# Weight gradients of the MLP run between the matmuls of the backward convolution, with the transposed tables and k^T kept in DRAM

## The chip, the cores and the metric

The kernel runs on one core of a Trainium2 chip. The time is the device time of one execution in microseconds (us), and runs are compared by their median.

## What is computed

Two layers are applied twice with the same weights: A, a gated long convolution, and B, an MLP. The kernel returns the output and the gradients for q, k, v, the short filter `shift_k`, the long filter `ssm_k`, `ssm_D`, and both weights and biases of the MLP.

```python
def _A_ref(q, k, v, shift_k, ssm_k, ssm_D):          # S = 2048, D = 512
    for t in range(4):
        k_shift = k_shift + k_pad[:, t:t + S, :] * shift_k[:, 3 - t][None, None, :]
    kv = k_shift * v
    y = irfft(rfft(pad(kv)) * rfft(pad(ssm_k)))[:S]   # length 2S, along the sequence
    return q * (y + kv * ssm_D)
def _B_ref(x, w1, b1, w2, b2):                        # F = 1376
    return gelu(x @ w1 + b1) @ w2 + b2
x = A_q
x = x + _A_ref(layernorm(x), A_k, A_v, A_shift_k, A_ssm_k, A_ssm_D)
x = x + _B_ref(layernorm(x), B_w1, B_b1, B_w2, B_b2)  # both lines a second time
_out, _vjp = jax.vjp(_f, A_q, A_k, ..., B_b2);  _grads = _vjp(grad_out)
```

Both uses of A share k, v and the filters, so the convolved y is computed once, and its gradient (`gy`) is the sum over both layers. The weight gradients of the MLP are sums over both layers as well: dW2 = h^T G and dW1 = (gz^T n)^T, where h, gz, G and n are kept per layer.

## The kernel before

**Stages in order.** `phase_conv_forward` makes the cosine and sine tables (`tabN`, `tabF`), transforms the filter and kv in five groups of frequencies, multiplies the spectra and transforms back to `res.y`; it keeps the spectra in DRAM (`Hspec`, `KVspec`). `phase_mlp` runs the two layers forward and then backward in four slices of 512 rows, and leaves in DRAM the tiles h and gz of both layers (11 chunks of 128 by 2048) and the normed inputs n. It then calls `weight_grads`. Last comes `phase_conv_backward`.

**Weight gradients, L897 to L934.** Both n are loaded whole (`dw_n`, 2 MB each, L906). For each of 22 chunks the tile `dw_tm` of each layer is transposed by a DMA (L920) and 32 matmuls of 128x512 run into one accumulator (L925). ScalarE evicts it (L928). For dW1 the result is turned by a DMA transpose (L933) and stored. There are 704 matmuls in all, and nothing else runs on TensorE meanwhile.

**Backward convolution.** The gradient `gy` is folded on VectorE (L174 to L205) and transformed with 112 matmuls (L230, table `tabFb`). For each group the spectrum `Hb` is loaded, multiplied on VectorE (L242 to L251) and transformed back with the table `tabIb` (L278 and L281, 112 matmuls). The table is made by four DMA transposes (L481). `inv_blocks` (L295 to L309) combines the blocks on VectorE into `gkv`. A loop over four blocks of 512 rows multiplies by v and by the shifted k, stores the gradient of v, loads 64 shifted tiles `kj` of k (L549 to L554, 128 KB each), runs 64 matmuls `gw` for the gradient of the short filter (L557) and transposes gks on TensorE (L562, evicted at L565). 256 small matmuls `gk` (L581) give the gradient of k, stored tile by tile (L585). Then `tabG` comes by four DMA transposes (L594), GY is multiplied by `KVb`, 228 matmuls `gh` (L627 and L629) transform back, and `inv_blocks` and two more operations for each of four column chunks give the gradient of the long filter, stored at L649. The last store is the small `gdo` (L651).

**What sets the order.** Tiles come from pools; a scheduler places the instructions on each engine, and an engine takes its own in that order. All DMAs of these stages are issued from one queue, SyncE's (SP), in order: a DMA that waits for its data or its buffer holds back all that stand behind it. A pool that opens where another was closed waits for the last use of that memory.

## Time and profile before

| what | before |
|---|---|
| median of 3 runs | 1245.59 us (1244.38 to 1254.66) |
| profiled execution: time | 1254.15 us |
| profiled execution: span | 1252.4 us |
| mean granted clock of TensorE | 0.829 |
| PE busy in the span | 789.9 us (63%) |
| VectorE (DVE) busy | 672.1 us (54%) |
| ScalarE (ACT) busy | 433.3 us (35%) |
| DMA traffic | 191.07 MB, mean 153 GB/s |

Each execution is profiled with times of every instruction from the span's start. Of the profiled execution 1.75 us lie outside the span. The granted clock is a share of full speed: 0.50 and 1.00 stand for TensorE's two levels, 1.2 and 2.4 GHz. The DMA share of a stretch is the mean busy share of the core's 16 DMA engines; it can exceed 1 a little at the edges of a short stretch.

### The profile page before, as it was taken

The numbers are of one execution on the slowest core, as the hardware profiler recorded it, in microseconds if no ns is written. First come the engines' busy times: TensorE is split into PE (matmuls) and PEld (weight loads), VectorE is DVE, ScalarE is ACT, GpSimd is POOL, SyncE is SP. The second block draws the span as 40 slices with busy tenths as digits, with TensorE's granted clock in tenths as the row PEclk, the third lists the DMA queues.
The fourth block names the chain that finished last, engine by engine and source line by source line (L and its number), as shares of the span: only waits on it lengthen the run. The fifth ranks groups of instructions, "written<-read, shape, count | busy, mean of one in ns | idle before, by whom it ended". The sixth has DMA issues, their size and how long they took to land. (4 is left out here: it accounts for less than half of the span.)

```text
span 1252.4 us, 10780 instructions
## 1 busy us (share of the span) xinstructions
PE 789.9 (63%) x3765; PEld 353.5 (28%) x3765; DVE 672.1 (54%) x1316; ACT 433.3 (35%) x538; POOL 97.5 (8%) x173
## 2 busy tenths in 40 slices
...
GB/s 193 138 227 165 172 163 69 79 146 113 135 143 147 155 143 193 185 202 207 206 233 169 168 131 44 220 173 171 172 189 133 159 118 34 135 244 219 140 18 50
DMA packets 308402, 191.07 MB, mean 153 GB/s; under 512 B 192814, under 2 KB 299260, under 8 KB 307964
## 3 DMA queue, kind: packets, MB, share of 16 engines
...
## 5 line engine op out<-in xcount | busy, mean ns | idle before, releaser
L816 PE MATMUL o_ps<-w_sb,h_sl 128*128 128x512 bf16 x352 | 96.0, 415 | 33.6 <-DVE h_sl L785 33.6
L925 PE MATMUL dw_ps<-G,dw_tm 128*128 128x512 bf16 x352 | 80.3, 393 | 42.2 <-issue 36.4
L257 DVE COPY spec_rb<-Hb 128x512 bf16<-128x512 bf16 x1 | 0.3, 294 | 197.6 <-DMA Hb<-Hspec_d 197.6
L925 PEld LDWEIGHTS <-dw_tm 128*128 128x128 bf16 x704 | 69.6, 99 | 128.8 <-issue 42.3
L835 PE MATMUL gh_ps<-gT_sl,w2T_sb 128*128 128x512 bf16 x352 | 85.0, 394 | 20.1 <-DMA gT_sl<-G 16.4
L803 PE MATMUL z_ps<-nT_sl,w_sb 128*128 128x512 bf16 x352 | 82.9, 390 | 19.5 <-DMA nT_sl<-n_sl 19.1
L846 PE MATMUL gn_ps<-w1T_sb,gz_sl 128*128 128x512 bf16 x352 | 83.5, 384 | 0.0
L891 ACT ACTIVATE nb_sl<-nb_sl,ab_ab 128x512 bf16<-128x512 bf16 x32 | 23.4, 802 | 152.5 <-DVE bb_junk L849 116.8
L925 PE MATMUL dw_ps<-dw_n,dw_tm 128*128 128x512 bf16 x352 | 76.1, 379 | 0.0
L928 ACT ACTIVATE dw_o<-dw_ps 128x512 bf16<-128x512 f32 x22 | 13.1, 597 | 181.9 <-PE dw_ps L925 181.9
L837 DVE SCALAR_TENSOR_TENSOR gz_sl<-gh_ps,gpb 128x512 bf16<-128x512 f32 x88 | 58.5, 689 | 25.9 <-DMA gpb<-gp_d 17.8
L805 ACT ACTIVATE g_z<-z_ps,b1col 128x512 bf16<-128x512 f32 x88 | 54.3, 691 | 19.8 <-PE z_ps L803 19.7
L816 PEld LDWEIGHTS <-h_sl 128*128 128x128 bf16 x352 | 33.8, 104 | 85.4 <-DVE h_sl L785 40.1
L813 PE MATMUL o_ps<-x_sl,ident 128*128 128x512 bf16 x32 | 13.3, 414 | 67.3 <-DVE x_sl L762 64.2
L835 PEld LDWEIGHTS <-w2T_sb 128*128 128x128 bf16 x352 | 35.4, 101 | 64.7 <-DMA gT_sl<-G 15.3
L803 PEld LDWEIGHTS <-w_sb 128*128 128x128 bf16 x352 | 34.8, 100 | 65.0 <-issue 16.7
L739 ACT ACTIVATE n_sl<-x_sl,ln_nmr,rstd 128x512 bf16<-128x512 bf16 x32 | 24.7, 820 | 70.0 <-POOL ln_nmr L732 70.0
L557 PE MATMUL gw<-kj,gks 128*128 128x512 bf16 x64 | 26.5, 561 | 32.9 <-DMA kj<-kB_d 20.6
L846 PEld LDWEIGHTS <-gz_sl 128*128 128x128 bf16 x352 | 34.7, 99 | 40.6 <-issue 2.0
L781 ACT ACTIVATE g_s<-g_t 128x2048 bf16<-128x2048 bf16 (+1 forms) x24 | 42.5, 1772 | 9.3 <-DVE g_t L780 9.3
L778 ACT ACTIVATE g_q<-g_z 128x2048 bf16<-128x2048 bf16 (+1 forms) x24 | 42.9, 1787 | 0.1
L278 PE MATMUL iv_ps<-Yg,tabI 128*128 128x512 bf16 x56 | 19.5, 453 | 36.7 <-DVE Yg L243 33.2
...
## 6 DMA issues: line engine op xcount, KB each, us to landing
...
```

What stands on the lines that cost most here:

```text
L557: nc.tensor.matmul(gw[cc], lhsT=gks[:, 4 * i + h, cs], rhs=kj[:, :, cs], start=(i == 0 and h == 0), stop=(i == 3 and h == 3))
L739: nc.scalar.activation(out=n[:, t, :], in_=x[:, t, :], func=ACT.Identity, bias=nmr[:, t:t + 1], scale=rstd[:, t:t + 1])
L778: nc.scalar.activation(out=q, in_=zb, func=ACT.Square)
L781: nc.scalar.activation(out=sg, in_=t, func=ACT.Sigmoid)
L803: nc.tensor.matmul(ps, lhsT=w.w1[:, dc, c * P:(c + 1) * P], rhs=nT[:, dc, :], start=(dc == 0), stop=(dc == ND - 1))
L805: nc.scalar.activation(out=zb[:, c - c0, :], in_=ps, func=ACT.Identity, bias=w.b1col[:, c:c + 1])
L816: nc.tensor.matmul(ps, lhsT=h[:, c, t * P:(t + 1) * P], rhs=w.w2[:, c, :], start=False, stop=(c == NFC - 1))
L835: nc.tensor.matmul(ps, lhsT=w.w2T[:, dc, c * P:(c + 1) * P], rhs=gT[:, dc, :], start=(dc == 0), stop=(dc == ND - 1))
L837: nc.vector.scalar_tensor_tensor(out=gz[:, c, :], in0=ps, scalar=1.0, in1=gp[:, c - c0, :], op0=ALU.mult, op1=ALU.mult, accum_out=m.b1part ...
L846: nc.tensor.matmul(ps, lhsT=gz[:, c, t * P:(t + 1) * P], rhs=w.w1T[:, c, :], start=(c == 0), stop=(c == NFC - 1))
L891: nc.scalar.activation(out=n[:, t, :], in_=n[:, t, :], func=ACT.Identity, scale=ab[:, 1, t:t + 1], bias=ab[:, 0, t:t + 1])
L925: nc.tensor.matmul(ps, lhsT=tm[:, i, t, :], rhs=rhs, start=(i == 0 and t == 0), stop=(i == 1 and t == NT - 1))
```

## The change

`weight_grads` becomes a generator, `fill`. It yields after each matmul with an estimate of that matmul's length. `conv_backward`, now a generator too, yields a number (`slack`) at places where TensorE would stand idle, and the driver then takes as many steps of `fill` as fit in it. What is left at the end runs after the convolution. TensorE's instructions of this part are wrapped so that the scheduler keeps them in the written order (`Ordered`).

The other parts of the change are these. The filler's tiles `dw_tm` are now one layer's each, with three buffers for each layer, and are fetched five ahead. n is loaded into G's memory once G has been used, so that the order of the work is all dW2 first. The transpose at the end of dW1 is four 128x128 matmuls and a second eviction. In the forward convolution the tables `tabI` and `tabG` and the transpose of k are written to DRAM, the last two by way of `res.y`'s memory. The backward part loads `tabIb`, `tabG` and `kTc` from there. The gradient of the short filter is 16 fused multiply-and-sum operations of 128x2048 on VectorE, and the 64 loads `kj`, the flipped copy `kB` and the 64 matmuls `gw` are gone. All DMAs of the backward convolution are issued from the GpSimd (Pool) queue, and SP keeps those of the weight gradients. `inv_blocks` works in place with two temporaries. The products by KV are made for all groups first, in place in GY, and `gh` runs column chunk by column chunk. Stores of gk are four tiles at a time.

```diff
...
-    flip_rows(nc, dram.kB, aps["A_k"].flatten_outer_dims(), 511, n=259)
     with ExitStack() as res.gystack:
-        phase_mlp(nc, tc, dims, consts, dram, res, aps)
+        m = phase_mlp(nc, tc, dims, consts, dram, res, aps)
         res.ystack.close()
         unflip_rows(nc, aps["out_0"].flatten_outer_dims(), dram.o0B)
         unflip_rows(nc, aps["out_1"].flatten_outer_dims(), dram.o1B)
-        phase_conv_backward(nc, tc, dims, consts, dram, res, aps)
+        dw = open_weight_grads(tc, res.gystack)
+        with ExitStack() as cst:
+            nc = Ordered(nc, tc, ("tensor",))
+            fill = weight_grads(nc, m, dims, aps, dw)
+            room = 0.0
+            for slack in conv_backward(cst, nc, tc, dims, consts, dram, res, aps):
+                room += slack
+                while room > 0.0:
+                    step = next(fill, None)
+                    room = room - step if step else 0.0
+            for _ in fill:
+                pass
...
+    nc.sync.dma_start(out=dram.tabI, in_=tabI)
+    tabG = res.y[:, :, :].rearrange("p (f k a) (b q) -> p f (k a b) q", f=2, a=1, q=256)
+    load_inverse_table(nc, tabG, dram.tabN)
+    nc.sync.dma_start(out=dram.tabG, in_=tabG)
+    kTn = res.y[:, :, :].rearrange("p (c t) d -> p c (t d)", c=ND)
+    for cc in range(ND):
+        nc.sync.dma_start_transpose(out=kTn[:, cc, :], in_=k_ap[:, cc * P:(cc + 1) * P])
+    nc.sync.dma_start(out=dram.kT, in_=kTn)
...
-def inv_blocks(nc, pool, W, N, last=False):
+def inv_blocks(nc, W, PN, MW, last=False):
 
     tt = nc.vector.tensor_tensor
-    G, B0, B1, PN, MW = [pool.tile([P, 2, 2, 512], BF16, name=f"ib{x}", tag=f"ib{x}", bufs=1)[:, :, :, 0:N]
-                         for x in range(5)]
     tt(out=PN, in0=W[:, :, 4:6], in1=W[:, :, 6:8], op=ALU.add)
     tt(out=MW, in0=W[:, :, 4:6], in1=W[:, :, 6:8], op=ALU.subtract)
+    G, B0, B1 = W[:, :, 4:6], W[:, :, 6:8], W[:, :, 2:4]
...
+    dma = nc.gpsimd.dma_start
...
-        nc.sync.dma_start(out=tabF, in_=dram.tabF)
+        dma(out=tabF, in_=dram.tabF)
         gyv = res.gy_bf[:, :, :].rearrange("p (i h) d -> p i (h d)", i=4)
         fg = Fold(nc, tp, gyv[:, :, 0:2 * D], gyv[:, :, 2 * D:4 * D], False)
+        yield 24.0
         for g, (k1, base, n) in enumerate(GROUPS):
             fwd_group(nc, psum, tabF, fg.streams(k1), g, GY[g])
...
+    tmp = res.gy_bf[:, :, :].rearrange("p (x a b) d -> p x a b d", x=4, a=2)
...
+        with tc.tile_pool(name="cb_rot", bufs=1, side="right") as rot:
+            tabI = rot.tile([P, 2, 16, 256], BF16, name="tabIb")
+            dma(out=tabI, in_=dram.tabI)
+            for g, (k1, base, n) in enumerate(GROUPS):
+                H = gyp.tile([P, 2, 4, 512], BF16, name="Hb", tag="Sg", bufs=2)
+                dma(out=H[:, :, 0:n, :], in_=dram.Hspec[:, :, base:base + n, :])
+                Rb = spec_second(nc, rot, H) if g == 0 else None
+                Y = rot.tile([P, 2, 4, 512], BF16, name="Yb", tag="Yg", bufs=1)
+                product(nc, rot, GY[g], H, Rb, g, Y, True)
+                yield 12.0 if g == 0 else 3.5
+                inv_group(nc, psum, tabI, Y, g, W)
         for m in range(2):
-            inv_blocks(nc, wp, W[m], 512)
-            tt(out=gkvv[:, :, m], in0=W[m][:, 0, 0:4], in1=W[m][:, 1, 0:4], op=ALU.add)
-            tt(out=gkvv[:, :, 2 + m], in0=W[m][:, 0, 0:4], in1=W[m][:, 1, 0:4], op=ALU.subtract)
-        wstack.close()
-        iostack = ExitStack()
-        io = iostack.enter_context(tc.tile_pool(name="cb_io", bufs=1))
-        gw = [psum.tile([P, 4, P], F32, name=f"gw{cc}", tag=f"gw{cc}", bufs=1) for cc in range(ND)]
-        gT = io.tile([P, ND, S + 16], BF16, name="gksT")
-        nc.vector.memset(gT[:, :, S:S + 16], 0.0)
-        for i in range(4):
-            sl = slice(4 * i, 4 * i + 4)
-            vb = io.tile([P, 4, D], BF16, name="vb", tag="vb", bufs=2)
-            tok_io(nc, vb, v_ap, dram.vB, i)
-            ksb = io.tile([P, 4, D], BF16, name="ksb_b", tag="ksb", bufs=2)
-            nc.sync.dma_start(out=ksb, in_=dram.ks[:, sl, :])
-            tt(out=gks[:, sl, :], in0=gkv[:, sl, :], in1=vb, op=ALU.mult)
-            tt(out=ksb, in0=gkv[:, sl, :], in1=ksb, op=ALU.mult)
-            tok_io(nc, ksb, out3, dram.o3B, i, store=True)
-            for h in range(4):
-                kj = io.tile([P, 4, D], BF16, name="kj", tag="kj", bufs=2)
+            inv_blocks(nc, W[m], tmp[:, 2 * m], tmp[:, 2 * m + 1])
+            tt(out=W[m][:, 0, 4:8], in0=W[m][:, 0, 0:4], in1=W[m][:, 1, 0:4], op=ALU.add)
+            tt(out=W[m][:, 1, 4:8], in0=W[m][:, 0, 0:4], in1=W[m][:, 1, 0:4], op=ALU.subtract)
+            yield 16.0
...
+                tok_io(nc, vb, v_ap, dram.vB, i, eng=nc.gpsimd)
+                ksb = io.tile([P, 4, D], BF16, name="ksb_b", tag="ksb", bufs=2)
+                dma(out=ksb, in_=dram.ks[:, 4 * i:4 * i + 4, :])
+                for h in range(4):
+                    gkv = W[h % 2][:, h // 2, 4 + i, :]
+                    tt(out=ksb[:, h, :], in0=gkv, in1=ksb[:, h, :], op=ALU.mult)
+                    tt(out=gkv, in0=gkv, in1=vb[:, h, :], op=ALU.mult)
...
+                yield 3.0
...
+                    dma(out=out2[(t - 3) * P:(t + 1) * P, :].rearrange("(t p) d -> p t d", p=P), in_=go)
+            gwo = io.tile([P, ND, 4], F32, name="gwo", tag="gwo", bufs=1)
+            junk = W[0][:, 0, 0:4, :].rearrange("p a d -> p (a d)")
+            for cc in range(ND):
...
+            for cc in range(ND):
+                kc = gyp.tile([P, 4096], BF16, name="kTc", tag="Sg", bufs=2)
+                nc.vector.memset(kc[:, 0:16], 0.0)
+                dma(out=kc[:, 16:16 + S], in_=dram.kT[:, cc, :])
...
-                for cc in range(ND):
-                    cs = slice(cc * P, (cc + 1) * P)
-                    nc.tensor.matmul(gw[cc], lhsT=gks[:, 4 * i + h, cs], rhs=kj[:, :, cs],
-                                     start=(i == 0 and h == 0), stop=(i == 3 and h == 3))
...
+                    nc.vector.scalar_tensor_tensor(out=junk, in0=gT[:, cc, 0:S], scalar=1.0,
+                                                   in1=kc[:, 16 - j:16 - j + S], op0=ALU.mult, op1=ALU.mult,
+                                                   accum_out=gwo[:, cc, j:j + 1])
+                    yield 1.6
+            gwb = wp.tile([P, ND, 4], BF16, name="gwb", tag="gwb", bufs=1)
+            nc.vector.tensor_copy(out=gwb, in_=gwo)
+            nc.scalar.dma_start(out=out4.rearrange("(c p) j -> p c j", p=P), in_=gwb)
...
-        for f in range(2):
-            for qt in range(2):
-                nc.sync.dma_start_transpose(out=tabG[:, f, :, qt * P:(qt + 1) * P], in_=dram.tabN[:, f, qt, :])
+        dma(out=tabG[:, :, :, 0:256], in_=dram.tabG)
...
+            KV = gyp.tile([P, 2, 4, 512], BF16, name="KVb", tag="Sg", bufs=2)
+            dma(out=KV[:, :, 0:n, :], in_=dram.KVspec[:, :, base:base + n, :])
+            Rb = spec_second(nc, hp, KV) if g == 0 else None
+            product(nc, hp, GY[g], KV, Rb, g, GY[g], True)
+            yield 1.3 * n
+        gdo = hp.tile([P, ND], BF16, name="gdo")
+        for cc in range(ND):
+            cs = slice(cc * P, (cc + 1) * P)
+            w = hp.tile([P, 2, 8, NQP], BF16, name="Wh", tag="Wh", bufs=2)
+            for g, (k1, base, n) in enumerate(GROUPS):
...
-            nc.sync.dma_start(out=out5[cc * P:(cc + 1) * P, :], in_=gh)
+            dma(out=out5[cc * P:(cc + 1) * P, :], in_=gh)
...
-        for i, l in ((0, 3), (1, 1)):
-            nc.sync.dma_start(out=nres[:, i, :, :], in_=m.n_d[l].rearrange("(t p) d -> p t d", p=P))
...
+    units = []
+    for which in range(2):
+        cs = list(range(NFC))
+        groups = [cs[:3]] + [[c] for c in cs[3:]] if which else [[c] for c in cs[:-3]] + [cs[-3:]]
+        for g in groups:
+            units += [(which, i, c) for i in range(2) for c in g]
+    tms, pss, late = {}, {}, []
+
+    def fetch(k):
+        which, i, c = units[k]
+        tms[k] = d.tp.tile([P, NT, P], BF16, name="dw_tm", tag=f"dw_tm{i}")
+        nc.sync.dma_start_transpose(out=tms[k], in_=(m.gz_d if which else m.h_d)[layers[i]][:, c, :])
+
+    def flush():
...
+    ahead = 5
+    for k in range(ahead):
+        fetch(k)
...
+    for k, (which, i, c) in enumerate(units):
+        if k + ahead < len(units):
+            fetch(k + ahead)
+        flush()
+        if which == 1 and (k == 0 or units[k - 1][0] == 0):
+            nc.sync.dma_start(out=m.G[1], in_=m.n_d[1].rearrange("(t p) d -> p t d", p=P))
+        f0, fcs = dims.FC[c]
+        if i == 0:
+            pss[c] = d.pp.tile([P, D], F32, name="dw_ps", tag="dw_ps")
+        ps, tm = pss[c], tms.pop(k)
+        for t in range(NT):
+            nc.tensor.matmul(ps, lhsT=tm[:, t, :], rhs=m.G[i][:, t, :], start=(i == 0 and t == 0),
+                             stop=(i == 1 and t == NT - 1))
+            yield 0.23
+        if which == 0 and i == 0 and c == NFC - 1:
+            nc.sync.dma_start(out=m.G[0], in_=m.n_d[3].rearrange("(t p) d -> p t d", p=P))
+        if i == 0:
+            continue
+        o = d.evp.tile([P, D], BF16, name="dw_o", tag="dw_o")
+        nc.scalar.activation(out=o, in_=ps, func=ACT.Identity)
+        if which == 0:
+            late.append((o[0:fcs, :], out9[f0:f0 + fcs, :]))
+        else:
+            pt = d.pp.tile([P, ND, P], F32, name="dw_pt", tag="dw_ps")
+            for dc in range(ND):
+                nc.tensor.matmul(pt[:, dc, :], lhsT=o[:, dc * P:(dc + 1) * P], rhs=m.ident, start=True, stop=True)
+            oT = d.evp.tile([P, ND, P], BF16, name="dw_oT", tag="dw_oT")
+            nc.scalar.activation(out=oT, in_=pt, func=ACT.Identity)
+            late.append((oT[:, :, 0:fcs], out7[:, f0:f0 + fcs].rearrange("(c p) f -> p c f", p=P)))
+            yield 0.3
...
```

Three places show how the order moves. The first is SP's queue in the forward convolution, where the inverse transform of kv needs `tabI` and, group by group, the filter's spectrum `Hg`; before:

```order
L481 DMA_TRANSPOSE tabI<-tabF_d 128x16x128 x4
L460 DMA Hg_997<-Hspec_d 128x2x1024
L463 DMA KVspec_d<-KVg 256x1x1024
L460 DMA Hg_1041<-Hspec_d 128x2x1024
L460 DMA Hg_1079<-Hspec_d 128x2x2048
L463 DMA KVspec_d<-KVg 256x1x1024
L460 DMA Hg_1182<-Hspec_d 128x2x2048
L463 DMA KVspec_d<-KVg 256x1x2048
L460 DMA Hg_1291<-Hspec_d 128x2x2048
L463 DMA KVspec_d<-KVg 256x1x2048 x2
L675 DMA w_sb<-in_B_w_dram 128x4x1376
```

And in the changed kernel (`y_res` is the memory of `res.y`, used as a buffer):

```order
L491 DMA tabI_d<-tabI 128x8192
L526 DMA_TRANSPOSE y_res<-tabN_d 128x16x128 x3
L507 DMA KVspec_d<-KVg 256x1x1024
L504 DMA Hg_1054<-Hspec_d 128x2x1024
L494 DMA tabG_d<-y_res 128x8192
L507 DMA KVspec_d<-KVg 256x1x1024
L504 DMA Hg_1092<-Hspec_d 128x2x2048
L497 DMA_TRANSPOSE y_res<-in_A_k_dram 128x2048 x4
L507 DMA KVspec_d<-KVg 256x1x2048
L498 DMA kT_d<-y_res 128x8192
L504 DMA Hg_1195<-Hspec_d 128x2x2048
L504 DMA Hg_1304<-Hspec_d 128x2x2048
```

Eleven transposes and stores that were not there stand on this queue; of the loads `Hg`, the first now goes ahead of the table (row 33 of the queue, not shown), and the later ones stand behind the transposes and stores of the two copies.

The second place is TensorE at the first inverse transform of the backward convolution (`iv_ps`). Before, it follows the forward transform (`sp_ps`) directly:

```order
L230 LDWEIGHTS tabFb
L230 MATMUL sp_ps<-fold_t,tabFb 128x512
L230 LDWEIGHTS tabFb
L230 MATMUL sp_ps<-fold_t,tabFb 128x512
L278 LDWEIGHTS tabIb
L278 MATMUL iv_ps<-Yb,tabIb 128x512
L278 LDWEIGHTS tabIb
L278 MATMUL iv_ps<-Yb,tabIb 128x512
```

In the changed kernel matmuls of the weight gradients (`dw_ps`, with G of one layer) stand before and after each group's inverse transform; here at its beginning:

```order
L55 LDWEIGHTS dw_tm
L55 MATMUL dw_ps<-G_3480,dw_tm 128x512
L55 LDWEIGHTS dw_tm
L55 MATMUL dw_ps<-G_3480,dw_tm 128x512
L55 LDWEIGHTS tabIb
L55 MATMUL iv_ps<-Yb,tabIb 128x512
L55 LDWEIGHTS tabIb
L55 MATMUL iv_ps<-Yb,tabIb 128x512
```

Every weight gradient matmul stood ahead of the backward convolution; now 73 of them stand ahead of its forward transform and 52 behind it, 61 between the five inverse groups, 139 behind the last of these, 52 between the transposes of gks, 194 between `gk` and `gh`, and 133 between and behind the four column chunks of `gh`.

The third place is where the gradient of k is stored and the last stage's loads are issued. Before, on SP's queue:

```order
L153 DMA out_dram<-o3B_d 4x256x512
L554 DMA kj<-kB_d 128x512 x4
L585 DMA out_dram<-gk_o 128x512 x3
L612 DMA KVb<-KVspec_d 128x2x2048
L585 DMA out_dram<-gk_o 128x512 x2
L612 DMA KVb<-KVspec_d 128x2x2048
L585 DMA out_dram<-gk_o 128x512 x3
L576 DMA out_dram<-gwb 128x4x4
L585 DMA out_dram<-gk_o 128x512 x3
L612 DMA KVb<-KVspec_d 128x2x2048
L585 DMA out_dram<-gk_o 128x512 x5
L594 DMA_TRANSPOSE tabG<-tabN_d 128x16x128 x4
```

In the changed kernel these stand on the Pool queue:

```order
L199 DMA out_dram<-ksb_b 128x2x512
L199 DMA o3B_d<-ksb_b 128x2x512
L199 DMA out_dram<-ksb_b 128x2x512
L199 DMA o3B_d<-ksb_b 128x2x512
L189 DMA out_dram<-o3B_d 4x256x512
L604 DMA out_dram<-gk_o 128x4x512 x2
L610 DMA kTc<-kT_d 128x2048 x2
L604 DMA out_dram<-gk_o 128x4x512 x2
L641 DMA KVb<-KVspec_d 128x2x1024 x2
L624 DMA tabG<-tabG_d 128x32x256
L634 IOTA nyq_i 1x272
L641 DMA KVb<-KVspec_d 128x2x2048 x3
```

The loads `kj` are gone, four loads `kTc` have come, each behind the VectorE work that frees its buffer, and the loads `KVb` and the plain load of `tabG` stand behind them.

## Rows read from the trace of the kernel before

**Rows 1.** Stretches: start:end, length, busy time of each engine, PE clock, DMA share, GB/s.

```profile
774.00:1236.00 462.00, 291.80 (x1540) 146.20 (x1540) 149.82 (x276) 83.76 (x136) 0.35 (x1) 0.80 0.62 147
790.00:805.00 15.00, 0.00 (x0) 0.00 (x0) 0.00 (x0) 0.00 (x0) 0.00 (x0) 0.50 1.06 307
850.00:900.00 50.00, 50.00 (x234) 22.64 (x232) 0.00 (x0) 4.68 (x8) 0.00 (x0) 1.00 0.81 170
900.00:950.00 50.00, 50.00 (x233) 22.64 (x232) 0.00 (x0) 4.18 (x7) 0.00 (x0) 1.00 0.99 190
972.00:1236.00 264.00, 135.52 (x836) 76.56 (x836) 149.41 (x275) 70.63 (x114) 0.35 (x1) 0.72 0.43 129
1050.00:1100.00 50.00, 12.22 (x55) 5.53 (x54) 33.08 (x44) 5.38 (x10) 0.00 (x0) 0.60 0.36 108
1100.00:1150.00 50.00, 27.83 (x160) 13.78 (x158) 5.34 (x5) 7.20 (x13) 0.00 (x0) 0.64 0.68 212
1236.00:1252.00 16.00, 0.00 (x0) 0.00 (x0) 0.00 (x0) 0.00 (x0) 0.00 (x0) 0.50 0.10 33
```

**Rows 2.** Groups of instructions from 740: line, form, count, busy, mean ns, idle before.

```profile
L925 PE MATMUL dw_ps<-G,dw_tm 128*128 128x512 bf16 x352 | 80.3, 393 | 42.2 <-issue 36.4 <-DMA dw_tm<-h_d 5.7
L925 PE MATMUL dw_ps<-dw_n,dw_tm 128*128 128x512 bf16 x352 | 76.1, 379 | 0.0
...
L557 PE MATMUL gw<-kj,gks 128*128 128x512 bf16 x64 | 26.5, 561 | 32.9 <-DMA kj<-kB_d 20.6 <-DMA kj<-in_A_k_dram 12.2
...
L627 PE MATMUL gh_ps<-tabG,Yh 128*128 128x257 bf16 x112 | 19.0, 288 | 12.9 <-DMA tabG<-tabN_d 12.4 <-ACT Wh L632 0.5
...
L581 PE MATMUL gk_ps<-wdiag_b,gksT 128*128 128x128 bf16 x256 | 18.5, 239 | 3.3 <-ACT gk_o L584 3.1 <-ACT gksT L565 0.2
...
L278 PE MATMUL iv_ps<-Yb,tabIb 128*128 128x512 bf16 x56 | 16.1, 404 | 8.9 <-DMA tabIb<-tabF_d 7.5 <-ACT Wb L284 1.4
...
L928 ACT ACTIVATE dw_o<-dw_ps 128x512 bf16<-128x512 f32 x22 | 13.1, 597 | 181.9 <-PE dw_ps L925 181.9
...
L250 DVE TENSOR_TENSOR pr_u<-GY,Hb 128x1024 bf16<-128x1024 bf16 x8 | 5.5, 690 | 0.0
...
L882 DVE SCALAR_TENSOR_TENSOR ab_u<-g_sl,ab_u 128x512 bf16<-128x512 bf16 x8 | 5.5, 688 | 0.0
...
L174 DVE TENSOR_TENSOR fold_x<-gy_bf 128x4096 bf16<-128x4096 bf16 x1 | 2.3, 2292 | 2.1 <-DMA out_dram<-dw_oT 2.1
```

**Rows 3.** SP's queue in order of time: start, length, issue, count.

```profile
775.10 15.59 SPq L906 DMA_DIRECT2D dw_n<-n_d  x2
790.73 24.34 SPq L920 DMA_TRANSPOSE dw_tm<-h_d  x6
...
1013.84 10.51 SPq L481 DMA_TRANSPOSE tabIb<-tabF_d  x4
...
1173.24 9.14 SPq L594 DMA_TRANSPOSE tabG<-tabN_d  x4
1214.30 21.45 SPq L649 DMA_DIRECT2D out_dram<-gh  x4
1235.86 0.38 SPq L651 DMA_DIRECT2D out_dram<-gdo  x1
```

**Rows 4.** The page, its groups: VectorE's longest idle time.

```profile
L257 DVE COPY spec_rb<-Hb 128x512 bf16<-128x512 bf16 x1 | 0.3, 294 | 197.6 <-DMA Hb<-Hspec_d 197.6
```

**Rows 5.** Stretches of the forward convolution, columns as in the first group.

```profile
139.00:156.00 17.00, 0.00 (x0) 0.00 (x0) 0.41 (x1) 1.00 (x1) 0.00 (x0) 0.60 1.08 212
...
170.00:190.00 20.00, 14.12 (x50) 5.22 (x51) 12.82 (x20) 6.14 (x6) 0.00 (x0) 0.83 0.38 136
190.00:210.00 20.00, 17.42 (x66) 6.85 (x65) 9.59 (x14) 8.31 (x10) 0.00 (x0) 0.84 0.25 101
210.00:224.00 14.00, 12.67 (x58) 5.32 (x57) 4.31 (x7) 8.31 (x10) 0.00 (x0) 0.98 0.00 1
```

**Rows 6.** Waits of SP's queue: for what, in total, times, longest.

```profile
SPq L1071 <- DMA out_dram<-gdo: 11.5, 1, 11.5
```

207 lines of the change are left out of this document (88 added, 119 removed).

## The prediction, made before the changed kernel ran

> **What bounds the kernel now.** I read the stretches first, from the point where the MLP's backward part ends (774) to the last store (1236). In these 462 us TensorE works 291.8 us and VectorE 149.8 us, and the DMA share is 0.62 [rows 1]. No unit is full over the whole; each is full in its own part. From 790 to 805 nothing computes and the DMAs run at 307 GB/s. From 850 to 950 TensorE is full at the high clock (1.00), DMA 0.81 to 0.99, VectorE 0. From 972 on it is the other way: in 264 us TensorE is busy 135.5 us at a mean clock of 0.72, and DMA is at 0.43. From 1050 to 1100 VectorE works 33 us and TensorE 12, from 1100 to 1150 TensorE 28 and VectorE 5, the DMAs at 212 GB/s [rows 1]. VectorE's longest idle time, 197.6 us, is the whole stage of the weight gradients [rows 4]: its next work needs memory and SP's queue, which that stage holds. The groups say what TensorE waits for there: 36.4 us at the start of the weight gradients ("issue"), 32.9 us for the loads `kj`, 12.4 us for `tabG`, 7.5 us for `tabIb` [rows 2]. SP's queue explains the first: two loads of 2 MB take 15.6 us before the first transpose is issued [rows 3]. So the tail is two stages in series, one full on TensorE and DMA, one a chain of waits with half of TensorE free.
>
> **What the change removes and adds, in work.** One weight gradient matmul costs 76.1/352 = 0.216 us at the high clock [rows 2]; 704 cost 152 us. The backward convolution's matmuls at that rate: 224 of 128x512 (forward and inverse) 48 us, `gk` 18.5 us at most [rows 2], `gt` 4 (64 with a quarter of the columns), `gh` some 25 (228 with half), the new turn of dW1 44 small ones, 3 us, and the sums for b2, 32 matmuls, 7: together 257 us, where 291.8 stand now. Gone are 64 `gw`, 26.5 us [rows 2]. TensorE waits 11 times for an eviction (0.60 us by L928 [rows 2]) before it turns dW1: 7 us. So TensorE alone would need about 265 us.
>
> VectorE gets 16 multiply-and-sums of 128x2048, for which no row stands. The nearest: the same operation on 128x512 takes 688 ns, a plain product of 128x1024 690 and of 128x4096 2292 [rows 2]. From the last two a plain product costs 0.155 us and 0.52 ns an element; the fused one then 1.04 ns an element, or 2.29 us for 2048. At the plain product's rate it would be 1.22 us, at four times the short one 2.75. I take 2.37 with the read of the sum: 38 us, between 20 and 44. VectorE has 149.8 + 38 = 188 us, still far below the tail.
>
> DMA: from 850 to 900, 234 matmuls use 14.6 transposed tiles, at a share of 0.81, so 2.8 us of all engines a tile, its stores with it; 44 tiles are 122 us. The loads of n cost 16 us (15 us at 1.06), the stores of the last MLP slices some 10. The convolution's own are 0.43 x 264 = 114 us [rows 1], less 64 `kj` (8 MB, about 26 us at 212 GB/s and share 0.68 [rows 1]), and with the table transposes (10.5 + 9.1 us [rows 3]) turned to plain loads of 2 MB, some 7 us each at 307 GB/s, plus 2 MB `kTc`: about 90. In sum some 240 us. This is close under the length that I get below; DMA isn't the bound, but every load will land late.
>
> **The chain of the changed tail, step by step from 774** (before's clock of the span). Fold and `tabFb`: five operations of 2.3 us [rows 2] make 12 us; the load of 2 MB shares the DMAs with five transposes and the last stores, and both are in after 23 us, at 797, with the sums for b2 and 73 weight gradient matmuls (23 us) as cover. Forward transform 112 x 0.216 = 24, to 821. `tabIb` can only be loaded when the forward transform leaves its memory: 7 us alone, double in company; 16, of which 52 matmuls (11 us) are cover: 837. The inverse transform and 61 matmuls, 37: 874. `inv_blocks`, two sets of six operations of 128x2048 and nine of 128x1024, about 27 us of VectorE, is covered by 139 matmuls, 30: 905. Four blocks of gks, each 16 small and 13 large matmuls (4 us) and a wait of some 7 us for the third and fourth block's loads, whose buffers come free late: 30, to 935. From here two routes run side by side: TensorE does `gk` (18.5 and some 5 waiting for stores), 194 matmuls, seven turns with their evictions, 48: 1006. VectorE does the multiply-and-sums, 38, and the products by KV, 31 (eight of 128x2048, some thirty of 128x1024), with some 10 us waiting because each `KVb` waits for a buffer that `kTc` or an earlier product holds, and `tabG` stands ahead of three of them on Pool's queue: 1014. The first column chunk ends just behind that, 1016. Three more, each 57 `gh` (6.3 us) and 29 matmuls (6.3): 38, to 1054. The last eviction, `inv_blocks` on the short rows (7 us: four stores stand 21.45/3 apart [rows 3]) and the store of `gh` (about 5): 14, to 1068. The remaining 46 matmuls and two turns take 12 and are done by then.
>
> Behind the last work 16.4 us stay: the store `gdo` goes at 1235.9 and its end is waited for 11.5 us [rows 3, 6]; the span ends at 1252.4. That gives 1084. For landings that come later than I have put them, with DMA at 80 per cent of the tail, I add 10.
>
> **The front pays.** Between 139 and 156 the DMAs are at 1.08 and TensorE idle, waiting for the first four transposes; after it their share falls to 0.38, 0.25 and 0.00, with TensorE at 14 of 20, 17 of 20 and 13 of 14 us [rows 5]. There is room for the work added: four transposes of a table like the first (15 us), four of k, three stores of 2 MB (7 us each at 307 GB/s, 10 at 212), about 50 us of DMA. But it stands on SP's queue ahead of loads `Hg` that the chain needs. The second `Hg` goes behind the four new transposes, some 15 us later, and the first now ahead of the table, some 3 earlier. Bounds: 0 (all in the gaps) and 50 (all in series). I take 10, because the gaps after 170 hold it and what TensorE does there has slack only in the first two groups. The copy of the flipped k (1 MB) is gone, which is in the 10.
>
> Sum: 1084 + 10 + 10 = 1104 of span, 1.75 us around it: 1106, against the profiled 1254.15, 12 per cent less. That execution lies above the median of the runs shown, 1245.59, so the changed median may lie a few us lower; I say 1105.
>
> **A rule weighed against it.** The rows show DMA at 0.81 to 0.99 while the weight gradients run and at 0.43 in the convolution [rows 1]; two queues can fill that valley, but not raise the peak. The Trainium skill, "DMA: Bandwidth & Descriptors", section on issuing engines, says as much: DMAs from any engine run on the same 16 engines, and a second issuer saves only issue time. By it, the Pool queue speeds no load up, and the overlap pays in late landings. What that comes to, priced from rows, is rival (a).
>
> **Rivals.** (a) DMA is the bound. Transposes that share the engines with 2 MB loads land at half rate; `tabFb`, `tabIb`, the block loads, the `KVb` and the last tiles `dw_tm` each come 10 to 12 us later than in my chain, and since TensorE's order is fixed, nothing passes them: five places, +50, 1155. For it: 0.99 from 900 to 950. Against: the same rows keep TensorE full with it [rows 1].
> (b) TensorE alone bounds the tail: 774 + 265 + 14 + 16 and a front of 5 give 1074. For it: the filler is cut to the gaps. Against: at 1014 VectorE's route is already the longer.
> (c) The front costs 40 rather than 10, all else equal: 1136.
> (d) Slower. Pool's DMAs, some 45 where SP had them, each need Pool to make them up; if one costs Pool 4 us and they go one after another on the chain, that is 180 us and undoes the 150 saved; it decides from about 3.4 us apiece. SP issues in 0.3 to 0.6 us, and for Pool there is no row. 1265. Against: about a dozen stand on the chain, 48 us by that price. The Trainium skill, "SBUF — State Buffer", section on who interferes with whom, speaks for (d): DMAs issued from GpSimd are held up while VectorE runs copies or tensor-scalar operations in its fast modes; no run here has shown such a DMA yet.
> (e) The order holds TensorE so that the weight gradients hide nothing: each stage waits for the other's loads, the 36 us and the `kj` waits saved are lost to the front and to waits: 1240.
>
> **How the numbers follow.** My forecast (1080 to 1130) 0.50; (a) 0.20; (b) 0.12; (c) 0.11; (d) 0.04; (e) 0.03. 1065 to 1170 holds all of the forecast, (b) and (c), and three quarters of (a): about 0.85. A measurement can tell some 1 per cent, 12 us, from no change. Faster by more 0.93, within it 0.03, slower 0.04.
>
> **What would show it.** Right: TensorE above 80 per cent busy from 850 to 1050 with clock 1.00; multiply-and-sums of 2.3 to 2.4 us; first `gh` some 235 us behind the end of the MLP; DMA share 0.7 to 0.9 throughout. Front: the forward convolution ends at about 262 instead of 252. (a) shows as waits of TensorE for `tabIb`, `dw_tm` or `tabG` above 40 us in sum; (d) as DMAs of Pool that start long after what they wait for. Wrong would be a first matmul of the convolution later than 830, or a multiply-and-sum above 3 us.

## The result, and the profile after

The changed kernel takes 1144.26 us, median of 4 runs, against 1246.77 for the kernel before; the ratio is **0.915** (95% interval 0.909 to 0.920). The forecast was 1105 with a range of 1065 to 1170. The direction holds and the time lies inside the range, but the gain is 8.5 per cent where 11.4 was forecast: 39 us of the 141 expected did not come. The time lies outside the 1080 to 1130 to which the prediction gave one half; the wider range was there for rivals. The profiled execution took 1144.24 us, its span is 1142.4. The ratios here and below are of runs within 1.5 per cent of their kernel's fastest, which leaves out one of the changed kernel's four runs, one with all small stores together, and two of four each with the b1 gradient in rows alone and with more buffers.

The head of the page of the changed kernel, the busy time of each engine:

```profile
PE 767.5 (67%) x3745; PEld 345.7 (30%) x3745; DVE 706.6 (62%) x1353; ACT 439.4 (38%) x549; POOL 132.4 (12%) x221
```

The tail in stretches, columns as in [rows 1]: start:end, length, busy time of PE, PEld, DVE, ACT and POOL, PE clock, DMA share, GB/s. The last row is the whole tail; [rows 1] has 462 us there.

```profile
775.00:800.00 25.00, 9.82 (x35) 3.81 (x33) 1.34 (x2) 0.60 (x1) 1.69 (x2) 0.64 0.82 106
800.00:825.00 25.00, 11.34 (x39) 4.30 (x38) 11.46 (x8) 0.60 (x1) 0.58 (x1) 0.64 0.82 189
...
850.00:875.00 25.00, 21.36 (x93) 9.28 (x92) 12.75 (x21) 5.97 (x7) 1.96 (x3) 0.92 0.94 187
875.00:925.00 50.00, 50.00 (x227) 22.36 (x226) 33.04 (x47) 15.60 (x23) 6.34 (x10) 0.97 0.91 149
...
1075.00:1125.00 50.00, 46.15 (x305) 28.80 (x305) 29.88 (x68) 19.47 (x41) 1.67 (x3) 1.00 0.40 87
...
925.00:1075.00 150.00, 104.91 (x710) 58.55 (x708) 90.23 (x160) 32.31 (x59) 21.30 (x28) 0.86 1.13 223
775.00:1142.00 367.00, 269.83 (x1518) 138.29 (x1515) 184.83 (x313) 89.86 (x147) 34.83 (x49) 0.87 0.84 163
```

From 875 to 925 the change does what it says: TensorE is full at the high clock while VectorE works 33 us, where [rows 1] have 0. But the first 50 us have TensorE at 21 of 50, and from 925 to 1075 the DMA share is 1.13 with TensorE at 105 of 150. (The share adds up the times of all packets. Above 1 over a whole stretch, not only at the edges of a short one, it says that packets overlap in time on one engine, so that part of their time is waiting; it is not the use of the engines alone.)

The longest waits of TensorE and VectorE for a DMA from 755 to the end, with one of Pool's: total, times and longest. L55 is the helper that writes TensorE's order.

```profile
PE dw_ps L55 <- DMA dw_tm<-h_d: 42.9, 5, 15.2
DVE ksb_b L581 <- DMA ksb_b<-ks_d: 23.8, 3, 13.2
DVE fold_x L211 <- DMA o1B_d<-nb_sl: 23.7, 1, 23.7
POOL tabFb L543 <- DMA o1B_d<-nb_sl: 22.0, 1, 22.0
DVE tabG L629 <- DMA out_dram<-gwb: 11.8, 1, 11.8
DVE pr_t L279 <- DMA KVb<-KVspec_d: 9.1, 2, 8.8
PE dw_ps L55 <- DMA G<-n_d: 8.4, 1, 8.4
```

All seven lie before the first `gh`. Of TensorE's 42.9 us for `dw_tm`, 28.8 lie before 825, at the very start. The stations of the chain against the forecast:

| station | forecast | after | late by |
|---|---|---|---|
| forward transform begins | 797 | 824.9 | 28 |
| forward transform ends | 821 | 852.4 | 31 |
| inverse transform begins | 837 | 863.4 | 26 |
| inverse transform ends | 874 | 907.5 | 34 |
| turning of gks (`gt`) begins | 905 | 949.4 | 44 |
| first `gh` | 1016 | 1067.0 | 51 |
| last store of `gh` | 1068 | 1125.2 | 57 |
| end of the span | 1084 + 10 + 10 | 1142.4 | 38 |

So half of the delay is there at the first station, 10 us come between the inverse transform and `gt`, where TensorE waits 10 us for a `dw_tm` (926 to 936) and VectorE 9.5 us for a load of `ksb_b`, and 13 in the last third; the 20 us that the forecast held in reserve (late landings, front) take up the rest.

### The profile page after: what moved, and what is told of

It is laid out like the page before. It is cut to its first block, busy times and chain, and to the rows that moved or that the text cites. A ratio compares the mean times of both kernels' runs of the same rounds, so it can differ in the third digit from the quotient of the medians.

```text
span 1142.4 us, 10702 instructions
## 1 busy us (share of the span) xinstructions
PE 767.5 (67%) x3745; PEld 345.7 (30%) x3745; DVE 706.6 (62%) x1353; ACT 439.4 (38%) x549; POOL 132.4 (12%) x221
## 4 chain that ended last, share of the span: by engine, by line
PE 21%; DVE 20%; DMA 15%; SPq 6%; ACT 6%; issue 5%; POOL 3%; DVEq 0%; ACTq 0%; POOLq 0%
PE dw_ps L55 7%; PE gh_ps L867 4%; DMA nb_sl<-n_d 3%; DMA ksb_b<-ks_d 2%; DVE ln_st L757 2%; SPq L956 2%; PE iv_ps L55 2%; PE gh_ps L55 2%; PE sp_ps L55 2%; DMA dw_tm<-h_d 2%; DVE g_o L818 2%; DVE gz_sl L869 2%; DMA o3B_d<-ksb_b 2%; DMA out_dram<-dw_oT 1%; DVE bb_junk L912 1%
## 5 line engine op out<-in xcount | busy, mean ns | idle before, releaser
L55 PE MATMUL dw_ps<-G,dw_tm 128*128 128x512 bf16 x704 | 170.7, 402 | 57.8 <-DMA dw_tm<-h_d 42.9
L55 PEld LDWEIGHTS <-dw_tm 128*128 128x128 bf16 x704 | 71.2, 103 | 148.1 <-DMA dw_tm<-h_d 41.0
L612 DVE SCALAR_TENSOR_TENSOR Wb<-gksT,kTc 128x2048 bf16<-128x2048 bf16 x16 | 36.7, 2293 | 15.9 <-ACT gksT L589 13.7
L814 ACT ACTIVATE g_o<-g_t 128x2048 bf16<-128x2048 bf16 (+1 forms) x24 | 42.4, 1765 | 0.0
L757 DVE BATCH_NORM_STATS2 ln_st<-x_sl 128x6 f32<-128x512 bf16 x64 | 41.9, 668 | 0.1
```

The costliest lines, as they stand in the source:

```text
L55: return self.tc.keep_in_program_order(f(*args, **kwargs))
L612: nc.vector.scalar_tensor_tensor(out=junk, in0=gT[:, cc, 0:S], scalar=1.0, in1=kc[:, 16 - j:16 - j + S], op0=ALU.mult, op1=ALU.mult, accum ...
L757: nc.vector.bn_stats(out=st, in_=x[:, t, :])
L814: nc.scalar.activation(out=o, in_=t, func=ACT.Sigmoid, scale=-1.0)
```

## The experiments

My theory after the result: (1) the overlap works, and what is missing are late DMAs; (2) at the start it is one particular transfer, later the transposes `dw_tm`, which land late next to the convolution's loads. The rivals: that a second queue (Pool's) is itself the cost or the gain; that TensorE's fixed order costs; that VectorE's new multiply-and-sums set the time; that the front pays more than it seems. All ratios below are to the kernel before on the same chip, with a 95% interval; 1 per cent is 12.5 us. The changed kernel itself stands at 0.915 (0.909 to 0.920).

| kernel | ratio | interval |
|---|---|---|
| all weight gradients first | 0.984 | 0.980–0.989 |
| transposes as plain loads | 0.878 | 0.874–0.883 |
| convolution's DMAs on SP | 0.910 | 0.906–0.914 |
| order not pinned | 0.917 | 0.915–0.919 |
| no multiply-and-sums | 0.921 | 0.915–0.928 |
| last `out1` stores on Pool | 0.903 | 0.898–0.908 |
| b1 gradient stored in rows | 0.896 | 0.891–0.900 |
| the same edit on the kernel before | 0.991 | 0.988–0.993 |
| `gwb` and `gdo` stores | 0.904 | 0.899–0.908 |
| three DRAM copies in the kernel before | 1.015 | 1.012–1.019 |
| rows + `gwb`/`gdo` | 0.896 | 0.892–0.900 |
| the same with more buffers | 0.892 | 0.886–0.899 |

### Is the overlap worth what it seems? All weight gradients first

```diff
+            for _ in fill:
+                pass
```

The filler is run dry before the convolution begins; all else stays.

> The changed kernel with all 704 weight gradient matmuls placed ahead of the backward convolution, as before the change; all its other parts stay. If the overlap carries the gain (forecast): the matmuls, 152 us, stand alone again and only some of it is won back from loads that no longer share the DMAs, 1205 to 1240 us. Rival: the other parts (plain tables, no kj, two queues) carry most of it: 1150 to 1180.

0.984: placing the weight gradients among the convolution's matmuls is worth 7 per cent, 87 us. In its profile VectorE is idle from 850 to 950, as in [rows 1], the first `sp_ps` matmul starts at 991.9 and the first `gh` at 1161.8. All other parts of the change together (fewer loads, tables without transposes, Pool's queue, the added copies) leave 1.6 per cent. Rival (e) falls.

### Do the transposes land late beside the loads? Plain loads in their place

```diff
-        nc.sync.dma_start_transpose(out=tms[k], in_=(m.gz_d if which else m.h_d)[layers[i]][:, c, :])
+        nc.sync.dma_start(out=tms[k], in_=(m.gz_d if which else m.h_d)[layers[i]][:, c, :].rearrange("p (t q) -> p t q", q=P))
```

Each tile is loaded with the same bytes, not transposed, so the weight gradients dW1 and dW2 are not the reference's.

> The changed kernel with the 44 transposes of h and gz replaced by plain loads of the same 512 KB each, so the two weight gradients are computed from tiles that are not transposed. Theory A (transposes of small packets starve beside large loads): waits of TensorE for dw_tm fall from 49 us to under 10 and the last store comes 30 to 50 us earlier, 1095 to 1115 us. Theory B (bytes): the same bytes, so 1135 to 1150, with waits for dw_tm above 30 us. Theory D (the pinned order and the chain of the convolution set the time, not the transposes): waits for dw_tm go, but the time stays above 1130.

0.878, that is 45 us less than the changed kernel, the largest gain of any one edit here. It isn't the shortfall's size: the forecast counted transposes too, and the kernel before was not run with plain loads. The tile `dw_tm` in both kernels (duration on SP's queue: ns min/median/max), first of the changed kernel:

```profile
L956 SPq DMA_TRANSPOSE dw_tm<-h_d x22: 1968/2393/18658, 769.3 to 938.8; - x22
L956 SPq DMA_TRANSPOSE dw_tm<-gz_d x22: 1853/3668/16588, 941.5 to 1089.9; - x22
...
  PE dw_ps L55: 49.4, 6
```

The same view with plain loads:

```profile
L956 SPq DMA_DIRECT2D dw_tm<-h_d x22: 319/320/12651, 768.9 to 898.5; - x22
L956 SPq DMA_DIRECT2D dw_tm<-gz_d x22: 319/320/3127, 901.9 to 1041.7; - x22
...
  PE dw_ps L55: 14.2, 3
```

The third line of each is TensorE's wait for the tile: it falls from 49 to 14 us. The DMA view of the two tails says why: queue (q1 is SP's, q0 the one that Pool feeds), packets, MB, and packet time as a share of 16 engines, of the changed kernel from 775 to 1142:

```profile
q1 hardware_dynamic: 102414, 30.76, 57.1%
q0 software_dynamic: 7824, 28.85, 27.1%
```

and with plain loads from 773 to 1096:

```profile
q1 hardware_dynamic: 20530, 30.66, 31.2%
q0 software_dynamic: 7824, 28.85, 25.0%
```

The bytes are the same. The packets of SP's queue take 0.571 x 367 = 210 us of all engines with transposes and 0.312 x 323 = 101 us without; Pool's take 99 and 81. For 44 tiles the difference is 2.5 us a tile. How much of it is the company shows in the kernel with all weight gradients first, where the same transposes run for the most part without the convolution's loads; its tail from 775 to 1237:

```profile
q1 hardware_dynamic: 105990, 31.67, 34.9%
q0 software_dynamic: 7824, 28.85, 18.6%
```

That is 0.349 x 462 = 161 us on SP's queue and 86 on Pool's. So of the 109 us some 60 are the transposes' even there, 1.4 us a tile; the other 49, and 13 on Pool's queue, come with the overlap. TensorE's wait is another matter: in that kernel it waits 35.1 us for `dw_tm`, all of it before 850, so most of the changed kernel's 49 us is not the price of the company either (below, on the start). The Trainium skill, "Advanced Engine Details and Errata", section on the X-Bar transpose, says that transposing DMAs are as fast as regular ones on trn2; these rows disagree, most of all for transposes that share the engines with loads.

### Is it Pool's queue? The convolution's DMAs back on SP

```diff
-    dma = nc.gpsimd.dma_start
+    dma = nc.sync.dma_start
```

and the same in the three calls that name the engine themselves.

> The changed kernel with the DMAs of the backward convolution issued from SyncE's queue again; all else as changed. Theory A (two queues side by side: the transposes of small packets get little of the DMA engines while a load with large packets from Pool's queue runs): with one queue no transpose takes over 6 us, where they take up to 18.7 us in the changed kernel; TensorE's waits for dw_tm fall from 49 us to under 15, and the waits move to the loads that now stand in line; 1125 to 1150 us against 1144. Theory B (the DMA engines simply have too many bytes to move): landings stay as late as they are, waits for dw_tm stay at 40 to 55 us, 1140 to 1150. Theory C (a queue of its own for the convolution is what makes the overlap work): over 1165.

0.910, its interval overlaps with that of the changed kernel. TensorE waits less for `dw_tm` (30.8 instead of 49.4 us; neither the 15 of theory A nor the 40 of theory B), the longest transpose takes 12.1 us instead of 18.7, but now the convolution's own loads stand behind the tiles on the one queue. Waits of the tail in that kernel, as above:

```profile
PE dw_ps L55 <- DMA dw_tm<-h_d: 30.8, 3, 14.1
DVE ksb_b L581 <- DMA ksb_b<-ks_d: 25.4, 1, 25.4
PE gt_ps L55 <- DVE Wb L582: 15.6, 2, 15.3
PE gh_ps L55 <- DVE GY L287: 10.4, 6, 3.4
```

So a second queue by itself neither gains nor costs anything that these runs can tell. Waits changed their place.

### Does the fixed order hold TensorE? Order not pinned

```diff
-            nc = Ordered(nc, tc, ("tensor",))
```

> The changed kernel without the fixed order on TensorE: the scheduler places the matmuls itself. It then puts no weight gradient matmul among the inverse groups and 261 ahead of most of gt. If the fixed order costs more than it gives (rival: a late tile holds back all that stands behind it): 1115 to 1138 us. If it is what makes the filler fill: 1150 to 1185.

0.917: no difference. The multiply-and-sums then wait 62.8 us for `gksT`, and TensorE waits 27.9 us for `dw_tm` instead of 42.9; the end is the same.

### Does VectorE set the time? No multiply-and-sums

```diff
+            nc.vector.memset(gwo, 0.0)
...
-                    nc.vector.scalar_tensor_tensor(out=junk, in0=gT[:, cc, 0:S], scalar=1.0,
-                                                   in1=kc[:, 16 - j:16 - j + S], op0=ALU.mult, op1=ALU.mult,
-                                                   accum_out=gwo[:, cc, j:j + 1])
```

The 16 sums, 36.7 us of VectorE, are left out, so the gradient of the convolution's weights (the output stored from `gwb`) is zero.

> The changed kernel without the 16 multiply-and-sums on VectorE: the gradient of the short filter is left at zero. If VectorE's route (multiply-and-sums, 38 us, then the products by KV) sets the first gh, as forecast: 20 to 35 us earlier, 1108 to 1125. If the loads of KVb and late tiles in TensorE's fixed order set it: 0 to 10 us, 1134 to 1145.

0.921: no gain at all. Its waits show 45 us of new idle time of VectorE, ahead of `tabG`:

```profile
DVE tabG L627 <- DMA out_dram<-gk_o: 45.3, 1, 45.3
```

and TensorE's rows in order of time (start, length) the last filler matmuls with the first `gh` right behind them:

```profile
1061.13 5.99 PE L55 MATMUL dw_ps<-G,dw_tm 128*128 128x512 bf16 x26
1066.96 0.38 PE L55 MATMUL gh_ps<-tabG,GY 128*128 128x257 bf16 x2
```

In the changed kernel the same two rows stand at 1061.22 and 1067.05. VectorE's last product by KV ends at 1056.5 there and at 1071.8 in the changed kernel, and the first `gh` starts at the same time: it comes when TensorE's written order gets there, with or without VectorE's 37 us.

### What is late at the start? The last `out1` stores on Pool, and the b1 gradient in rows

SP's queue of the changed kernel at the end of the MLP: start, length, issue.

```profile
769.32 4.63 SPq L956 DMA_TRANSPOSE dw_tm<-h_d  x2
774.04 0.54 SPq L1075 DMA_DIRECT2D out_dram<-b1o  x1
774.63 0.70 SPq L1078 DMA_DIRECT2D out_dram<-b1o  x1
775.39 16.23 SPq L956 DMA_TRANSPOSE dw_tm<-h_d  x1
791.72 1.05 SPq L199 DMA_DIRECT2D out_dram<-nb_sl  x1
792.87 1.46 SPq L199 DMA_DIRECT2D o1B_d<-nb_sl  x1
```

The last two stores of `out1`, for which the fold and `tabFb` wait, stand behind a transpose that takes 16 us to issue. Two edits: either the stores go to Pool's queue,

```diff
-                tok_io(nc, ret.pop(), out1, dram.o1B, s, store=True)
+                tok_io(nc, ret.pop(), out1, dram.o1B, s, store=True, eng=nc.gpsimd if s == NSL - 1 else None)
```

> The changed kernel with the two stores of the MLP's last slice issued from Pool's queue, ahead of its loads, so that they do not stand behind a transpose on SyncE's. Theory A' (the fold waits 23.7 us for that store, which is held up on SyncE's queue by a starved transpose): fold begins at about 780 instead of 799, the forward transform 10 to 20 us earlier, 1124 to 1136 us. Rival (TensorE's fixed order has 73 weight gradient matmuls ahead of the forward transform, and their starved tiles hold it to 820 to 825 anyway): 1138 to 1146.

or the column store of the b1 gradient, 1376 pieces of two bytes, is turned on TensorE first and goes out in 11 rows (the last, shorter row has a store of its own):

```diff
...
-            nc.sync.dma_start(out=out8[0:nfull * P].rearrange("(c p) -> p c", p=P), in_=b1o[:, 0:nfull])
...
+        nc.tensor.matmul(bps[0:NFC, 0:P], lhsT=b1o, rhs=m.ident, start=True, stop=True)
...
+        nc.scalar.activation(out=b1r, in_=bps[0:NFC, 0:P], func=ACT.Identity)
+        nc.sync.dma_start(out=out8[0:nfull * P].rearrange("(c p) -> c p", p=P), in_=b1r[0:nfull, :])
...
```

> The changed kernel with the gradient of b1 turned by one small matmul and stored as 11 rows, instead of as a column of 1376 two-byte pieces. Theory E (this store keeps the DMA engines busy for some 15 us just when the MLP ends, and the third transpose and the last out1 stores stand behind it): the third transpose takes under 6 us instead of 16.2, the fold starts before 787 instead of 799, 1118 to 1134 us. Rival, theory A (Pool's loads of Hb starve that transpose): it still takes over 10 us, fold at 794 or later, 1138 to 1146.

The first gives 0.903, 15 us less, but not by the way of theory A': the stores go at 779 and land late all the same (the fold waits 21.7 us for them), issued 2 us behind the column store of the b1 gradient; TensorE's wait for `dw_tm` falls to 27.1 us. The second gives 0.896, 24 us less (by the median of all four runs, 1127.36, it is 17), and SP's queue in its trace shows why:

```profile
769.32 6.94 SPq L956 DMA_TRANSPOSE dw_tm<-h_d  x3
776.31 0.58 SPq L199 DMA_DIRECT2D out_dram<-nb_sl  x1
776.93 0.47 SPq L199 DMA_DIRECT2D o1B_d<-nb_sl  x1
```

Without the column store three transposes take 6.9 us, the fold waits 8.3 instead of 23.7, TensorE waits 16.8 us for `dw_tm` instead of 49.4, and the forward transform starts at 809.0 instead of 824.9. That it is this store and not the transposing is seen in the kernel with plain loads as well, where the column store stands: there the last `out1` store is issued at 775.9, with no transpose ahead of it, and lands 18.5 us later. The same edit was made on the kernel before:

> The kernel before with the same one edit, the gradient of b1 stored as rows. Theory E: the two loads dw_n stand on SyncE's queue under 4 us instead of 15.6, the first weight gradient matmul comes at 790 to 796 instead of 805, and the time falls by 9 to 16 us. Rival (the loads themselves take that long): the first matmul stays at 803 or later and the time within 4 us.

0.991: 12 us there. It settles a reading of the prediction. I had put the 36 idle us of [rows 2] down to two loads of 2 MB that take 15.6 us [rows 3]. With the b1 gradient in rows the same two loads take 3.1 us on SP's queue, and the first weight gradient matmul starts at 789.9 instead of 805.2:

```profile
772.52 3.13 SPq L906 DMA_DIRECT2D dw_n<-n_d  x2
```

In the kernel before, the stretch in which they hung (as [rows 1]) has the DMA engines at a share above 1 with almost no bytes:

```profile
775.00:783.00 8.00, 0.00 (x0) 0.00 (x0) 0.00 (x0) 0.00 (x0) 0.00 (x0) 0.50 1.17 41
783.00:790.00 7.00, 0.00 (x0) 0.00 (x0) 0.00 (x0) 0.00 (x0) 0.00 (x0) 0.50 1.04 63
```

and with the edit 357 GB/s at a share of 1.09 from 775 to 783. The queue's packets, MB and packet time of the kernel before, from 770 to 775 and from 775 to 783, tell more:

```profile
q1 hardware_dynamic: 1410, 0.00, 12.7%
...
q1 hardware_dynamic: 328, 0.33, 117.5%
```

The store's own packets are all recorded before 775 and are brief, 0.6 us of all engines. The 328 behind them are packets of 1 KB, of other DMAs, and take 0.46 us each (8 us x 16 engines x 1.175 / 328); with the edit 2806 of them take 0.05 us each. So for some 15 us behind the column store, 2.7 KB, the engines move almost nothing; what they do in that time no view shows. It had been there to see in the stretches, had I cut them finer than at 790.

### The other small stores: `gwb` and `gdo`

```diff
-            gwb = wp.tile([P, ND, 4], BF16, name="gwb", tag="gwb", bufs=1)
+            gwb = gyp.tile([P, ND, 4], BF16, name="gwb", tag="gwb", bufs=1)
...
-            dma(out=out6.rearrange("(c p) -> p c", p=P), in_=gdo)
...
+        nc.tensor.matmul(ps[0:ND, 0, 0:P], lhsT=gdo, rhs=consts.ident, start=True, stop=True)
...
+        nc.scalar.activation(out=gdr, in_=ps[0:ND, 0, 0:P], func=ACT.Identity)
+        dma(out=out6.rearrange("(c p) -> c p", p=P), in_=gdr)
```

`gwb` moves to another pool, so that `tabG`'s memory does not wait for its store; the gradient of D, 512 pieces of two bytes, goes out in four rows.

> The changed kernel with two other small stores mended: gwb in memory that is not used again, and the last store gdo turned by one matmul and stored as 4 rows instead of 512 two-byte pieces. Theory E: VectorE's wait of 11.8 us for gwb goes, first gh 8 to 12 us earlier; the wait behind the last store falls from 10.8 us to about 3; together 1124 to 1133 us. Rival (first gh is set by late tiles dw_tm in TensorE's fixed order): only the end counts, 1134 to 1139.

0.904, 14 us less. The span ends 8 us behind the last store of `gh` (issued at 1117.2) instead of 17, since `gdo` lands 2.4 us after its issue instead of 14.9. The 11.8 us of VectorE for `gwb` are gone too, and the first `gh` comes at 1057.5, 9.5 us earlier. How the one leads to the other isn't shown: the run without the sums says that VectorE's route doesn't set the first `gh`, and what TensorE itself no longer waits for on its way there is a late `dw_tm` (6.5 us) and half of its waits for evictions.

### The front alone: three DRAM copies in the kernel before

```diff
+    nc.sync.dma_start(out=dram.tabI, in_=tabI)
...
+    load_inverse_table(nc, tabG, dram.tabN)
+    nc.sync.dma_start(out=dram.tabG, in_=tabG)
...
+    for cc in range(ND):
+        nc.sync.dma_start_transpose(out=kTn[:, cc, :], in_=k_ap[:, cc * P:(cc + 1) * P])
+    nc.sync.dma_start(out=dram.kT, in_=kTn)
```

> The kernel before with the three copies to DRAM added in the forward convolution (tabI, tabG, k^T), which nothing reads. The forecast put their price at 10 us, with bounds of 0 and 50. The traces of the two kernels put the end of the MLP at 774.2 and 775.8: if they are hidden, 1247 to 1254 us beside 1250; if their price is there but paid back elsewhere in the changed kernel: 1256 to 1270.

1.015: the added work costs 19 us. In the trace, of its fastest run, the span is 9.8 us longer than that of the kernel before, and 8.6 of them are there at the first MLP matmul: 322.0 against 313.4. In the changed kernel, which does the same work, it comes at 314.4. The tile `z_ps` in the first of these (durations, then first and last start):

```profile
L814 PE MATMUL z_ps<-nT_sl,w_sb x343: 376/379/634, 322.0 to 541.5; 128*128 128x512 bf16 x172
```

and in the changed kernel:

```profile
L835 PE MATMUL z_ps<-nT_sl,w_sb x352: 376/379/634, 314.4 to 533.5; 128*128 128x512 bf16 x176
```

Two things differ there: the changed kernel loads the first `Hg` ahead of the table's transposes, and it no longer copies the flipped k. The first can be seen in the stretches. In the changed kernel TensorE has work from 139 to 156, where [rows 5] and the kernel with the copies alone (up to 170) have none; the share of the second wasn't measured.

```profile
139.00:156.00 17.00, 6.49 (x16) 1.54 (x14) 1.75 (x4) 3.99 (x4) 0.00 (x0) 0.60 1.07 263
```

### All small stores together, and more buffers

The b1 gradient in rows with the edit of `gwb` and `gdo`; then the same with four buffers in place of two for the evictions of the weight gradients, a buffer of its own for the third `KVb`, and 12 in place of 24 us of filler ahead of the forward transform.

> The changed kernel with both edits on small stores: b1 as rows, and gwb and gdo as in the run on the end stores. Theory E (small pieces cost engine time at three separate places, the end of the MLP, the products by KV and the end): the gains of the two runs, some 17 us each, add up, 1105 to 1116 us. Rival (what one place gives back is lost at the next wait, for late tiles or loads): 1118 to 1128.

> The same with three more edits: four buffers for the evictions of the weight gradients instead of two, a buffer of its own for the third KVb so that it is loaded ahead, and 12 us instead of 24 of filler ahead of the forward transform. If the waits that the trace shows there (late tiles ahead of the forward transform, KVb behind kTc's buffers) still set the time: 5 to 15 us under the run with the two edits, 1092 to 1108. If the DMA engines are full in that stretch and only change places: within 4 us of it.

0.896 and 0.892. The two edits alone give 24 and 14 us, together 23; by the medians of all runs 17 and 17, together 23 (1120.81): they don't add. A place where gain is lost can be seen. In the first combination TensorE has a new wait:

```profile
PE dw_ps L55 <- DMA dw_tm<-gz_d: 17.1, 1, 17.1
```

SP's queue there shows four transposes in 48 us, behind the load of n on the same queue and beside `kTc`, `tabG`, `KVb` and the stores of gk on Pool's:

```profile
968.90 48.31 SPq L959 DMA_TRANSPOSE dw_tm<-gz_d  x4
```

The first `gh` comes at 1051.0 there and at 1036.2 with the b1 gradient in rows alone. Both combinations are faster than the changed kernel (their intervals end below its own), but none is measurably faster than the b1 gradient in rows alone.

## Why the prediction came out as it did

**The overlap.** Right. TensorE's work in the tail is 269.8 us, where the prediction had about 265; VectorE's 184.8, where it had 188; the clock where TensorE is full (875 to 925) is 0.95 to 1.00. The multiply-and-sum takes 2293 ns where I took 2.37 us:

```profile
L612 DVE SCALAR_TENSOR_TENSOR Wb<-gksT,kTc 128x2048 bf16<-128x2048 bf16 x16 | 36.7, 2293 | 15.9 <-ACT gksT L589 13.7
```

**Which route sets the first `gh`.** Wrong. I had VectorE's at 1014 ahead of TensorE's at 1006; the run without the sums shows that TensorE's order sets it (1067.0 in both).

**The start (797 forecast, 825 measured).** The largest single step that failed. "Both are in after 23 us" counted a load of 2 MB, five transposes and the last stores as sharing the engines, but not that those stores stand behind a transpose on SP's queue, nor that hardly anything lands for some 15 us behind the b1 store. I read the 15.6 us of [rows 3] as the price of the two loads, so it fell away with them in my sum; it belonged to a store that stays. Shown by the two runs with that edit: 24 us here, 12 in the kernel before.

**The price of a transposed tile.** The term that was mis-sized. I took 2.8 us of all engines, from a stretch in which transposes run alone, and 240 us for the whole tail. Measured are 0.84 x 367 = 308. Without the overlap my sum is right: 0.54 x 462 = 249 in the kernel with all weight gradients first. What it lacks is the company, some 60 us of packet time, most of it on the transposes. Against plain loads a tile costs 2.5 us more here, where my price left no more than about 1 us for transposing (a plain load of half a MB at 307 GB/s is 1.7 us). And I divided by the whole tail: "DMA isn't the bound" is right for 0.84 of 367 us and doubtful for the 150 us from 925 to 1075, at 1.13. From the end of the inverse transform to the first `gh` the delay grows by 17 us; that the DMAs set all of this isn't shown.

**Rival (a)** is what happened in part: transposes that share the engines with loads land late, and TensorE waits 49 us for `dw_tm`, above the 40 that I had named as its mark. But the mark doesn't tell (a) from the b1 store: 28.8 of the 49 lie before 825, and with the b1 gradient in rows 16.8 are left. It was priced at +50; the time is +39 over the forecast. It had the places wrong: the inverse table, for instance, was in sooner than in my sum (31 us late ahead of it, 26 behind it), while the small stores, which no rival names, cost 24 and 14 us when mended one at a time. So it is in part luck that the time lies in the range. (b) and (c) fall: TensorE works 270 of 367 us, and the front costs about 1.

**The marks that I named.** TensorE is busy 153.0 of 200 us from 850 to 1050, not above 80 per cent, at a mean clock of 0.89; the first `gh` comes 292 us behind the end of the MLP (775), not 235 (my own chain makes it 242, from 774 to 1016); the DMA share is 0.84, but from 0.38 (825 to 850) to 1.17 (975 to 1025) by stretch. The last write of the forward convolution's y starts at 255.9 instead of 252.8, not 10 us later; with the copies alone it starts at 261.3. The first matmul of the convolution (824.9) lies just under the 830 that would have been wrong.

**The reserve.** The front was to cost 10 and cost about 1; the copies cost 19 when they are added alone, of which the traces show 8.6 at the first MLP matmul, so the changed kernel wins most of that back in the front; the earlier `Hg` fits it, but wasn't tested alone. Late landings were to cost 10; the stations are 57 late, at the start and ahead of `gt` by landings. Behind the last work I put 16.4 us as before; it is 17.2, and SP still waits 10.8 us for `gdo`, the wait that [rows 6] show with 11.5:

```profile
SPq L1141 <- DMA out_dram<-gdo: 10.8, 1, 10.8
```

**Rival (d)**, Pool's DMAs at 4 us each, falls. (Its 1265 doesn't come out of its working: 1105 + 180 is 1285.) They take Pool 0.5 to 0.8 us, two of them 1.7 (`tabG` and the copy out of `o3B`), also while VectorE works:

```profile
852.89 0.53 POOL L555 DMA_DIRECT2D tabIb<-tabI_d  x1 [52.19 <-PE sp_ps L55]
856.40 0.71 POOL L558 DMA_DIRECT2D Hb<-Hspec_d  x1 [2.97 <-DVE pr_u L286]
```

The Trainium skill, "SBUF — State Buffer", section on who interferes with whom, would have such DMAs held up by VectorE's fast copies and tensor-scalar operations; here the idle times in brackets name what they waited for, and it was data or memory. That is a weak test of the rule: nearly all of VectorE's time in this tail goes to products and sums of two tensors, not to copies and tensor-scalar operations.

**What stays open.** How the 39 us divide: the edits' gains (45, 24 and 14 us) overlap, and plain loads and rows were not run together. Why a transposed tile is dearer in company: whether its small packets lose in taking turns with the loads' large ones, or the engines pay for each change between the two kinds. One stretch of the changed kernel shows how far it goes: from 853 to 877 these two queues had

```profile
q0 software_dynamic: 688, 4.19, 60.8%
q1 hardware_dynamic: 2578, 0.65, 47.8%
```

so 0.65 MB on SP's queue in 24 us, against 8.46 MB of transposes and their stores in 50 us when they are alone (the kernel before, 850 to 900). Putting both on one queue moved the waits and left the time, so it does not tell the two apart.
